# Loading the q and k weight chunks of a fused attention and FFN kernel as joint rows, with the first two tiles computed chunk by chunk over eight PSUM banks

## The chip, the cores and the metric

The kernel runs on one core of one Trainium2 chip (trn2). The metric is device time in microseconds (us); a lower time is better. Before the change it was 274.67 us (median of 3 runs, 274.52 to 274.93). The span in a profile, from the first to the last instruction, is about 1.3 us shorter than the device time of the same run (273.2 against 274.49 us for the kernel before).

Engines are named as the profile names them: PE is the TensorE matmul, PEld its weight load, DVE the vector engine, ACT the scalar engine, POOL GpSimd, SP the sync engine. SP and ACT each own a queue of loads ("SPq", "ACTq" in the profile when they issue one). The granted clock is the share of its full clock that PE is given, as the profile records it.

## The reference, cut to what matters

```python
# S = 2048, D = 640, H = 32 heads of 20, F = 1728
g = sigmoid((x * gate_w).sum(-1, keepdims=True))
q, k, v = split(x @ wqkv)                  # wqkv: 640 x 1920; q, k, v are 640 wide each
pq, pk = phi(q), phi(k)                    # phi(t) = where(t > 0, t + 1, exp(t)) + 1e-6
a = linear_attention(pq, pk, v) @ wo
b = (gelu(x @ w_gate) * (x @ w_up)) @ w_down
out = g * a + (1 - g) * b
```

The change touches only the start: the loads of the q and k columns of `wqkv`, and the products of the first two tiles (128 rows of x each) with them.

## The kernel before, as far as the change touches it

The 640 rows of `wqkv` are loaded in five chunks of 128 rows, and each matmul takes one chunk. A product of one tile with q or with k is a sum over five chunks, held in two banks of PSUM (the memory `ps`, where the results of PE go): 512 columns in one and 128 in the other. I call the two matmuls of one tile, one chunk and one of q or k a *step*; the first two tiles need 2 x 2 x 5 = 20 steps.

The loads before. k halves come first, chunk by chunk, with rows of 640 x 2 = 1280 bytes; q halves follow as two loads of two and three chunks:

```python
P.op("act", lambda e: e.dma_start(touch[0:16, 0:4], A_wqkv[0:128:8, 640:644]), ...)   # tiny "touch"
load_x(0)                # SP
load_wk(0)               # SP
load_x(1, "act")
load_wk(1)               # SP
load_wk(3)               # SP
...
load_wk(2, "act")
load_wk(4, "act")
...
dma_in(gw_sb[0:5, :], gate_w..., [r_gw], eng="act")     # gate weights, 1.2 KB
load_wq(0, 2)            # SP
load_wq(2, KC, "act")
for i in range(NXN, NT):                                # transposed x tiles 2 to 15, on SP
    load_xT(i, after=([r_wk[4]] if i == NXN else ()))
```

The products before: k of both tiles, in the order in which the chunks were expected, then q of both tiles.

```python
warm(5, 512); warm(1, 128)                 # matmuls on constants, to keep PE busy
T(0, [0], 7); T(0, [1, 2, 3, 4], 6)        # PE transposes of x tile 0
warm(6, 128)
KM(0, [0])                                 # step: k, tile 0, chunk 0
T(1, [0], 7); T(1, [1, 2, 3, 4], 6)
warm(3, 128)
KM(1, [0])
for k in (1, 3):
    KM(0, [k]); KM(1, [k])
gate_col()                                 # gate weights as an extra column of the q half
for k in (2, 4):
    KM(0, [k]); KM(1, [k])
for n in range(4):
    if n == 2:
        for k in range(3):
            QM(2, [k]); QM(3, [k])
        QM(2, [3, 4]); QM(3, [3, 4])
    phi1(n); phi2(n)                       # exp on ACT, then two operations on DVE
for i in range(2, NT):
    KQ(i)                                  # q and k of tiles 2 to 15
```

## Time and profile before

| what | before | read from |
|---|---|---|
| device time | 274.67 us | median of 3 runs |
| PE busy | 269.7 of 273.2 us | page, part 1 |
| PE waits after 11 us | none | waits of PE, window 11 us to the end |
| first matmul of KQ (tile 2) | 11.40 us | timeline of PE |
| chunk 3 of k lands, PE resumes | 6.96, 7.01 us | chain of waits, timeline |

From the page of the kernel before, its span, the busy times of part 1 and the shares of the chain that ended last:

```profile
span 273.2 us, 3449 instructions
...
PE 269.7 (99%) x1369; PEld 128.6 (47%) x1369; DVE 141.9 (52%) x251; ACT 76.0 (28%) x132; POOL 30.0 (11%) x28
...
PE 97%; DMA 2%; SPq 0%; DVE 0%; issue 0%
```

The kernel is PE-bound nearly from end to end. Only the head has idle PE time, and the chain that ended last shows what it waits for there. This is that chain in order of time (start, length, what):

```profile
2.21 4.76 DMA pool<-in_A_wqkv_dram
6.96 0.05 issue
7.01 0.39 PE ps L453
```

Up to 6.96 us the chain is a load of `wqkv`; from 7.01 us on it is PE without a break. The timeline of PE in the head (start, duration, operation; in brackets the idle time before it and what ended it):

```profile
4.62 0.38 PE L453 MATMUL ps<-pool 128*128 128x512 bf16 x1 [0.18 <-DMA pool<-in_A_wqkv_dram]
...
6.20 0.22 PE L454 MATMUL ps<-pool 128*128 128x128 bf16 x1
7.01 0.39 PE L453 MATMUL ps<-pool 128*128 128x512 bf16 x1 [0.59 <-DMA pool<-in_A_wqkv_dram]
7.23 0.22 PE L454 MATMUL ps<-pool 128*128 128x128 bf16 x1
7.29 0.38 PE L453 MATMUL ps<-pool 128*128 128x512 bf16 x1
...
11.40 0.81 PE L540 MATMUL ps<-pool 128*128 128x512 bf16 x3
```

L453 and L454 are the two matmuls of a k step. Steps start every 0.27 us (7.01, 7.29); the single durations are longer because matmuls overlap. There is one large wait, 0.59 us, for chunk 3 of k. The q steps that follow never wait. L540 is the first matmul of `KQ`. Since PE does not wait after it, its start decides the time.

### The profile page before, as it was taken

What the parts mean: (1) busy time and instruction counts of PE and PEld (TensorE: products, weight loads), DVE (VectorE), ACT (ScalarE), POOL (GpSimd) and SP (SyncE); (2) the same over time, 40 slices, a digit from 0 to 9 for tenths busy, and PEclk for the clock granted to TensorE, in tenths of its full rate; (3) what the DMA queues carried; (4) which work ended last, traced back from release to release, by engine and by line L of the source; (5) the groups of instructions that cost most, each with busy time, mean ns of one, the idle gap of its engine ahead of it and who ended that gap; (6) DMA issues with size and microseconds to landing.
All of it is one profiled execution on the core that took longest, in us unless ns stands there. A gap on an engine that the chain in (4) does not pass through costs nothing.

```text
span 273.2 us, 3449 instructions
## 1 busy us (share of the span) xinstructions
PE 269.7 (99%) x1369; PEld 128.6 (47%) x1369; DVE 141.9 (52%) x251; ACT 76.0 (28%) x132; POOL 30.0 (11%) x28
## 2 busy tenths in 40 slices
PE   7999999999999999999999999999999999999997
PEld 4555555544445444444444444444444444444444
DVE  2588989998234334999999999634210000000200
ACT  2355555310421454223222223224011121121021
POOL 5000000003240001242332422000000000000000
PEclk9999999999999999999999999999999999999999
DMA  6675999500300011522121221263031110110211
GB/s 207 179 118 122 322 402 386 143 3 12 65 19 2 23 49 51 182 45 48 26 48 24 48 42 34 60 215 109 5 77 38 41 38 19 38 41 19 58 58 41
DMA packets 42160, 23.61 MB, mean 86 GB/s; under 512 B 31519, under 2 KB 40735, under 8 KB 42015
## 3 DMA queue, kind: packets, MB, share of 16 engines
q1 hardware_dynamic: 41269, 22.40, 30.0%
q10 hardware_dynamic: 874, 0.98, 1.0%
q8 instruction: 11, 0.18, 0.3%
q14 instruction: 6, 0.05, 0.0%
HBM read 13.83 MB, written 2.63 MB: 60 GB/s over the span
## 4 chain that ended last, share of the span: by engine, by line
PE 97%; DMA 2%; SPq 0%; DVE 0%; issue 0%
PE ps L701 41%; PE ps L865 23%; PE ps L540 14%; PE ps L597 6%; PE ps L844 4%; DMA pool<-in_A_wqkv_dram 2%; PE ps L679 2%; PE ps L812 2%; PE ps L600 1%; PE ps L468 1%; PE ps L825 1%; PE ps L453 1%; PE ps L722 1%; PE ps L740 0%; SPq L340 0%; PE ps L469 0%
## 5 line engine op out<-in xcount | busy, mean ns | idle before, releaser
L701 PE MATMUL ps<-pool 128*128 128x512 bf16 x520 | 113.7, 379 | 0.0
L701 PEld LDWEIGHTS ps<-pool 128*128 128x128 bf16 x520 | 50.5, 98 | 60.0
L865 PE MATMUL ps<-pool 128*128 128x512 bf16 (+2 forms) x306 | 62.7, 367 | 0.0
L707 ACT ACTIVATE pool<-ps 128x512 f32<-128x512 f32 x52 | 31.0, 597 | 73.1 <-PE ps L701 73.1
L709 DVE TENSOR_TENSOR pool<-ps,pool 128x512 bf16<-128x512 f32 x52 | 34.7, 689 | 31.7 <-PE ps L701 30.4
L865 PEld LDWEIGHTS ps<-pool 128*128 128x128 bf16 x306 | 29.2, 98 | 33.4 <-issue 0.4
L540 PE MATMUL ps<-pool 128*128 128x512 bf16 (+1 forms) x210 | 38.1, 344 | 0.0
L848 DVE TENSOR_TENSOR pool<-ps,pool 128x512 bf16<-128x512 f32 x4 | 2.8, 692 | 61.5 <-PE ps L844 61.5
L755 POOL TENSOR_TENSOR pool<-pool 128x640 f32<-128x640 bf16 x16 | 22.5, 1406 | 72.9 <-DVE pool L757 66.2
L872 ACT ACTIVATE pool<-ps,pool 128x512 bf16<-128x512 f32 (+1 forms) x16 | 10.9, 681 | 68.6 <-PE ps L865 68.6
L540 PEld LDWEIGHTS ps<-pool 128*128 128x128 bf16 x210 | 20.5, 98 | 17.5
L559 DVE SCALAR_TENSOR_TENSOR pool<-ps,pool 128x128 bf16<-128x128 f32 (+2 forms) x42 | 25.3, 602 | 2.4
L550 ACT ACTIVATE pool<-ps 128x640 bf16<-128x640 f32 x28 | 19.7, 704 | 18.2 <-DVE pool L559 10.9
L597 PE MATMUL ps<-pool 128*128 128x512 bf16 x78 | 19.4, 379 | 0.0
L765 DVE TENSOR_TENSOR pool<-pool 128x640 bf16<-128x640 bf16 x16 | 13.2, 826 | 0.6
L763 DVE TENSOR_SCALAR pool<-pool 128x32 f32<-128x32 f32 x16 | 12.8, 802 | 0.6
L757 DVE TENSOR_REDUCE pool<-pool 128x32 f32<-128x640 f32 x16 | 12.9, 807 | 0.0
L645 DVE TENSOR_TENSOR pool<-pool 128x640 f32<-128x640 f32 x14 | 11.6, 825 | 0.5
L844 PE MATMUL ps<-pool 128*128 128x512 bf16 x52 | 11.6, 379 | 0.0
L647 POOL PARTITION_ALL_REDUCE pool<-pool x1 | 4.0, 3972 | 61.5 <-DVE pool L645 61.5
L597 PEld LDWEIGHTS ps<-pool 128*128 128x128 bf16 x78 | 7.0, 98 | 7.3
L556 DVE TENSOR_SCALAR pool<-pool 128x640 bf16<-128x640 bf16 x28 | 9.2, 327 | 1.8 <-ACT pool L550 0.3
(70 smaller groups left out, 105.8 us busy)
## 6 DMA issues: line engine op xcount, KB each, us to landing
out_dram<-pool SPq DMA_DIRECT2D x19, 128.0 KB, 1.7
pool<-in_B_w_gate_dram SPq DMA_DIRECT2D x1, 2080.0 KB, 13.8
pool<-in_B_w_up_dram SPq DMA_DIRECT2D x1, 2080.0 KB, 19.3
pool<-in_A_x_dram SPq DMA_DIRECT2D x1, 1280.0 KB, 8.6
pool<-in_B_w_down_dram SPq DMA_DIRECT2D x1, 1120.0 KB, 6.0
pool<-omg_row SPq DMA_DIRECT2D x1, 1024.0 KB, 4.8
pool<-in_A_x_dram SPq DMA_DIRECT2D x1, 960.0 KB, 5.7
pool<-in_A_wo_dram SPq DMA_DIRECT2D x6, 160.0 KB, 10.0
```

Source lines behind the costliest of these rows:

```text
L540: last = e.matmul(ps[:, b + p, 0:c1 - c0], xT[:, k, i * 128:(i + 1) * 128], wkq[:, k, c0:c1], start=(k == 0), stop=(k == KC - 1))
L550: P.op("act", lambda e: e.activation(e_buf[m], ps_flat[:, o:o + 640], ACT.Exp), reads=banks, writes=[r_e[m]])
L559: P.op("dve", lambda e, c0=c0, c1=c1: e.scalar_tensor_tensor(dst[:, c0:c1], ps_flat[:, o + c0:o + c1], 1.0 + EPS, e_buf[m][:, c0:c1], ALU. ...
L597: last = e.matmul(ps[:, b, :], pk[i][:, c * 128:(c + 1) * 128], x_aug[:, i, 0:512], start=(i == 0), stop=(i == NT - 1))
L701: last = e.matmul(ps[:, b, :], w[:, k, fc * 128:(fc + 1) * 128], xT[:, k, j * 512:(j + 1) * 512], start=(k == 0), stop=(k == KC - 1))
L707: P.op("act", lambda e: e.activation(ge[n], ps[:, gb, :], ACT.Gelu_apprx_tanh), reads=[bank[gb]], writes=[r_ge[n]])
L709: P.op("dve", lambda e: e.tensor_tensor(hT[fc][:, j * 512:(j + 1) * 512], ps[:, ub, :], ge[n], ALU.mult), reads=[bank[ub], r_ge[n]], write ...
L755: P.op("pool", lambda e: e.tensor_tensor(tmp[n], pq[i], z_b, ALU.mult), reads=[r_pq[i], r_zb], writes=[r_tmp[n]])
L757: P.op("dve", lambda e: e.tensor_reduce(den[n], tmp[n].rearrange("p (h d) -> p h d", h=32), AX.X, ALU.add), reads=[r_tmp[n]], writes=[r_de ...
L765: P.op("dve", lambda e: e.tensor_tensor(pq[i].rearrange("p (h d) -> p h d", h=32), pq[i].rearrange("p (h d) -> p h d", h=32), den[n].unsqu ...
L844: last = e.matmul(ps[:, b, :], wd[:, fc, 512:640], hT[fc][:, j * 512:(j + 1) * 512], start=False, stop=(fc == NFC - 2), skip_group_check=True)
L865: last = e.matmul(ps[:, pb, 0:c1 - c0], lhs, rhs, start=False, stop=(q == len(rows) - 1), skip_group_check=True)
```

## The change

The intent is to load q and k of a chunk together, as rows of 2560 bytes, so that fewer and longer rows are moved. Because q and k now arrive together, the first two tiles are computed chunk by chunk, with all four products open at once in all eight banks. A second tiny load, over chunks 1 to 4, is placed behind x tile 1 to touch that memory early. The gate load moves to the front, and the gate column moves from the q half to the k half. The core of the diff:

```diff
-            wk = wkq[:, :, 0:640]
-            wq = wkq[:, :, 640:1281]
+            wq = wkq[:, :, 0:640]
+            wk = wkq[:, :, 640:1281]
...
             load_x(0)
-            load_wk(0)
+            load_w(0, 640, 1280)
             load_x(1, "act")
-            load_wk(1)
-            load_wk(3)
+            P.op("act", lambda e: e.dma_start(touch[0:64, 4:8], A_wqkv[128:640:8, 640:644]), ...)
+            (the memset of gw_sb, moved here)
+            dma_in(gw_sb[0:5, :], gate_w.rearrange("(k p) -> k p", p=128), [r_gw], eng="act")
+            load_w(0, 0, 640)
+            load_w(1, 0, 1280)
+            load_w(3, 0, 1280)
...
-            load_wk(2, "act")
-            load_wk(4, "act")
-            dma_in(gw_sb[0:5, :], gate_w.rearrange("(k p) -> k p", p=128), [r_gw], eng="act")
-            load_wq(0, 2)
-            load_wq(2, KC, "act")
+            load_w(2, 0, 1280, "act")
+            load_w(4, 0, 1280, "act")
...
-                load_xT(i, after=([r_wk[4]] if i == NXN else ()))
+                load_xT(i, after=([r_wk[3]] if i == NXN else ()))
...
             warm(6, 128)
-            KM(0, [0])
+            PM(0, [0], tail=False)
             T(1, [0], 7)
             T(1, [1, 2, 3, 4], 6)
-            (warm(3, 128), then the k steps, the gate column and the q steps as above)
+            gate_col()
+            PM(1, [0], tail=False)
+            PM(0, [0], main=False)
+            PM(1, [0], main=False)
+            PM(2, [0])
+            PM(3, [0])
+            for n in range(4):
+                PM(n, [1])
             for n in range(4):
+                PM(n, [2])
+                PM(n, [3, 4])
                 phi1(n)
                 phi2(n)
```

`PM(n, ks)` does the steps of product n (k of tile 0, k of tile 1, q of tile 0, q of tile 1) over the chunks `ks`; "tail" is its second matmul, which for k also holds the gate column.

## The prediction

> **What bounds it now.** TensorE: the page gives PE 269.7 of 273.2 us, the chain of waits is 97% PE, and the waits of PE after 11 us are empty. The change acts only before that. What counts is the start of the first KQ matmul (L540, tile 2), 11.40 us in the timeline; any shift of it passes whole into the span.
>
> **The head now (timeline, and landings in the trace).** The first weight matmul is at 4.62 us (wk 0 lands at 4.49). 20 chunk steps (512 + 128 columns) follow at a pitch of 0.27 us, 5.4 us together. PE idles about 0.6 us, until 7.00, when wk 3 lands (6.96). wk 2 lands at 5.68, wk 4 at 7.16, the gate load at 7.35, wq 0-1 at 8.53, wq 2-4 at 9.39; wq is never late. So the order of now, wk first, hides most of the load. At most about 0.9 us is to be won.
>
> **What the change does.**
> - Rows of 2560 bytes. A 1280-byte packet takes 55 ns (median), a 3328-byte one of the later loads 133: about 6 ns fixed, so 2560 bytes should take 104 ns against 110. The Trainium skill (DMA: Bandwidth & Descriptors, "Why small descriptors are slow") names such a fixed cost; the trace agrees. On 1.3 MB that is about 0.2 us.
> - The second touch should take the long first packets (between 5.5 and 6.7 us many took 200 to 800 ns, and wk 3's last engine landed 1.0 us after its ninth). I count on half of that.
> - The gate load, ahead of the large loads, no longer lands at 7.35.
> - The cost: k and q of a chunk arrive together, so k is not served first. From 4.6 us 1.48 MB remain, as before. The same page ("Queues, rings and completion order") says that each engine alternates between queues; the trace shows both moving about equally from 3.3 to 5.5 us. At 350 to 380 KB/us (estimate from 332 now, less stalls and packet cost) the SP queue brings wq 0 at about 5.5, chunk 1 at 7.2, chunk 3 last at 8.6; the ACT queue chunk 2 at 6.5, chunk 4 at 8.3.
>
> **Critical path after.** Chunk 0's work ends at about 6.6 us. PE waits for chunk 1 until 7.2; from there 16 steps remain, 4.4 us: 11.6. From chunk 3's landing 11 remain, 3.0 us: 11.6. The transposed load of tile 2 starts when chunk 3 has landed, 8.6 instead of 7.17, and takes 2.95 us (measured now): 11.55, just in time. The release of banks 0 and 1 (1.9 us after a product's end now) comes at about 11.4. Four limits fall together; the latest decides: L540 starts at 11.5 to 11.9, estimate 11.65, 0.25 us later than now. Swapping the halves in KQ costs nothing: same matmuls, same vector work.
>
> **Prediction.** 274.67 + 0.25 = 274.9 us, 8 in 10 between 274.3 and 275.6. Faster by over 2%: 0.005; within 2%: 0.985; slower: 0.01.
>
> **What would show it.** Right: PE idle before chunk 1's matmuls (0.4 to 0.8 us) and again before chunk 3's or the first L540, released by DMA; after 12 us everything the same, shifted; the gate matmul no longer after the chunk 3 wait. Wrong: chunk 1 landing before 6.8 us or all chunks before 8.2 (all stalls gone), giving 274.3; or chunk 3 near 9.4 with the transposed load behind it, giving 275.5. A PE idle long enough to lower its granted clock (1.00 throughout now) would cost over 1 us; I give it 5%.

## The result

| | before | after |
|---|---|---|
| device time, median | 274.60 us (6 runs, 274.14 to 274.94) | 275.47 us (6 runs, 275.29 to 276.01) |
| span of the profiled run | 273.2 us | 274.0 us |
| first matmul of KQ | 11.40 us | 12.21 us |

The ratio of the runs is 1.0036 (95% interval 1.0021 to 1.0051). Ratios are the mean time of one kernel's fast runs over the mean time of the other's fast runs of the same rounds, so not quite the ratio of the medians quoted. The change made the kernel slower by 0.36%, which is about 1.0 us, clear of the noise though inside the band of 2%. A second measurement of the same kernel on another occasion gave 1.0036 again (below).

The page after, the same lines:

```profile
span 274.0 us, 3444 instructions
...
PE 270.5 (99%) x1366; PEld 128.7 (47%) x1366; DVE 141.8 (52%) x251; ACT 76.2 (28%) x132; POOL 30.0 (11%) x28
...
PE 96%; DMA 2%; ACTq 1%; ACT 0%; issue 0%; DVE 0%
```

The chain that ended last, after, in order of time:

```profile
3.46 5.62 DMA pool<-in_A_wqkv_dram
9.08 0.14 issue
9.22 0.38 PE ps L455
```

The load that the chain hangs on now lands at 9.08 us instead of 6.96. The timeline of PE, after (L455 and L457 are the two matmuls of a step, L524 is the first of KQ, L487 makes the gate column):

```profile
5.55 0.19 PE L487 MATMUL ps<-pool 128*128 128x5 bf16 x1 [0.20 <-DMA pool<-in_gate_w_dram]
5.60 0.59 PE L455 MATMUL ps<-pool 128*128 128x512 bf16 x1
...
7.09 0.39 PE L455 MATMUL ps<-pool 128*128 128x512 bf16 x1
...
8.40 0.39 PE L455 MATMUL ps<-pool 128*128 128x512 bf16 x1
8.62 0.22 PE L457 MATMUL ps<-pool 128*128 128x129 bf16 x1
9.22 0.38 PE L455 MATMUL ps<-pool 128*128 128x512 bf16 x1 [0.38 <-DMA pool<-in_A_wqkv_dram]
...
12.21 2.10 PE L524 MATMUL ps<-pool 128*128 128x512 bf16 x9
```

PE waits for the gate weights (5.55), for chunk 1 (7.09), for chunk 2 (8.40, one step) and for chunk 4 (9.22). From 9.22 us on it is gapless, and 11 of the 20 steps are still to be done: 12.21 - 9.22 = 2.99 us.

The matmul at 5.60 took 0.59 us, where those of the kernel before took 0.38 from 4.62 us on: PE was still at half pace. In all fourteen profiles the first matmuls of 512 columns start every 0.43 us and later ones every 0.22. The pace doubles at 4.2 us in the kernel before, at about 6.3 us in the changed kernel, and between 3.9 (e9) and 9.8 us (e3) in the other runs, although the windows view gives a granted clock of 1.00 from the start. This did not decide the time here: in the second profile of the changed kernel PE was at full pace from 4.7 us on, and KQ started later still (12.47 us), because the last landing decided.

When each load landed, from the completion records in the trace (us; a load is complete when the last of its sixteen shares has landed). "After, again" is the second profile of the changed kernel:

| load | before | after | after, again |
|---|---|---|---|
| chunk 0 | k 4.49 | k 4.08, q 4.84 | k 4.08, q 4.77 |
| chunk 1 | k 5.46 | 7.05 | 7.56 |
| chunk 2 | k 5.68 | 8.35 | 8.36 |
| chunk 3 | k 6.96 | 8.34 | 9.06 |
| chunk 4 | k 7.16 | 9.08 | 9.34 |
| gate weights | 7.35 | 5.51 | 6.33 |
| q chunks 0 and 1 | 8.53 | with the chunks | with the chunks |
| q chunks 2 to 4 | 9.39 | with the chunks | with the chunks |

This table holds the explanation to be tested. The last byte came a little *sooner* after the change (9.08 against 9.39 us). But before, when the last load (q 2 to 4) landed, PE was still working on q chunks 0 and 1, with only 6 steps to go from 9.76 us, and did not wait. After, 11 steps stood behind the last landing.

### The profile page after: what moved, and what is told of

It is laid out like the page before. It is cut to its first block, busy times and chain, and to the rows that moved or that the text cites. A ratio compares the mean times of both kernels' runs of the same rounds, so it can differ in the third digit from the quotient of the medians.

```text
span 274.0 us, 3444 instructions
## 1 busy us (share of the span) xinstructions
PE 270.5 (99%) x1366; PEld 128.7 (47%) x1366; DVE 141.8 (52%) x251; ACT 76.2 (28%) x132; POOL 30.0 (11%) x28
## 4 chain that ended last, share of the span: by engine, by line
PE 96%; DMA 2%; ACTq 1%; ACT 0%; issue 0%; DVE 0%
PE ps L685 41%; PE ps L849 23%; PE ps L524 14%; PE ps L581 6%; PE ps L828 4%; DMA pool<-in_A_wqkv_dram 2%; PE ps L796 2%; PE ps L663 2%; PE ps L584 1%; PE ps L455 1%; PE ps L809 1%; PE ps L706 1%; PE ps L724 0%; ACTq L340 0%; PE ps L457 0%; ACTq L360 0%
## 5 line engine op out<-in xcount | busy, mean ns | idle before, releaser
L524 PE MATMUL ps<-pool 128*128 128x512 bf16 (+1 forms) x210 | 38.1, 344 | 0.0
L524 PEld LDWEIGHTS ps<-pool 128*128 128x128 bf16 x210 | 20.5, 98 | 17.5
L629 DVE TENSOR_TENSOR pool<-pool 128x640 f32<-128x640 f32 x14 | 11.6, 826 | 0.5
L828 PE MATMUL ps<-pool 128*128 128x512 bf16 x52 | 11.6, 379 | 0.0
```

The source lines that it names most:

```text
L524: last = e.matmul(ps[:, b + p, 0:c1 - c0], xT[:, k, i * 128:(i + 1) * 128], wkq[:, k, c0:c1], start=(k == 0), stop=(k == KC - 1))
L828: last = e.matmul(ps[:, b, :], wd[:, fc, 512:640], hT[fc][:, j * 512:(j + 1) * 512], start=False, stop=(fc == NFC - 2), skip_group_check=True)
```

## The experiments

Theory A: the cost is the arrival order. With q and k of a chunk in one load, no product can finish its sum before nearly all bytes have come, so too many steps are left behind the last landing. Its rivals: B, the small loads early on the ACT queue delay chunks 2 and 4; C, the release of banks or the transposed load of tile 2 is the limit; D, long rows stall more; E, the eight-bank order itself costs.

Each experiment was timed over 5 rounds against the kernel before on the same chip (4 to 6 runs of each). The table gives the ratio to the kernel before and, for the profiled run, the start of the first KQ matmul and the span.

| run | edited from | ratio (95% interval) | KQ starts | span |
|---|---|---|---|---|
| changed kernel | | 1.0036 (1.0021 to 1.0051) | 12.21 | 274.0 |
| after_again | after, unchanged | 1.0036 (1.0020 to 1.0052) | 12.47 | 274.2 |
| e1_no_touch2 | after | 1.0066 (1.0037 to 1.0095) | 15.03 | 276.8 |
| e2_pool_small | after | 1.0121 (1.0106 to 1.0135) | 15.04 | 276.8 |
| e3_chunk2_all | after | 1.0054 (1.0035 to 1.0073) | 13.90 | 275.7 |
| e4_half_rows | after | 1.0038 (1.0026 to 1.0050) | 12.52 | 274.3 |
| e5_k_then_q | after | 1.0090 (1.0061 to 1.0118) | 12.00 | 273.8 |
| e9_k_first | after | 1.0011 (0.9998 to 1.0024) | 11.60 | 273.4 |
| e10_small_sp | after | 1.0069 (1.0048 to 1.0089) | 12.63 | 274.4 |
| e7_before_touch2 | before | 1.0029 (1.0013 to 1.0044) | 12.03 | 273.9 |
| e6_before_k_order | before | 0.9990 (0.9978 to 1.0001) | 11.18 | 272.9 |
| e8_before_q_single | before | 0.9970 (0.9955 to 0.9984) | 11.71 | 273.5 |
| e12_q_single_only | before | 0.9993 (0.9979 to 1.0007) | 10.81 | 272.6 |

One thing can be read from the last two columns at once. From the first KQ matmul to the end, all fourteen profiles (these and the kernel before) take 261.7 to 261.9 us, however the head went. So everything that separates these kernels happens before KQ, and it passes whole into the time. A profile is one run; where the runs of a kernel differ among themselves, its ratio counts and its profile shows only how that one run went. The profiles of e1, e3 and e8 are of runs near or at the slow end of their kernel (278.02, 276.92 and 274.85 us, medians 275.98, 276.13 and 273.90), that of e5 is of its fastest (275.00, median 277.43).

### Undoing the grouping of the loads (e9_k_first)

```diff
-            load_w(0, 0, 640)
-            load_w(1, 0, 1280)
-            load_w(3, 0, 1280)
+            load_w(1, 640, 1280)
+            load_w(3, 640, 1280)
...
-            load_w(2, 0, 1280, "act")
-            load_w(4, 0, 1280, "act")
+            load_w(2, 640, 1280, "act")
+            load_w(4, 640, 1280, "act")
+            (then q chunks 0 and 1 on SP, q chunks 2 to 4 on ACT)
...
             (PE: the k steps over chunks 1, 3, 2, 4, then the q steps, as before the change)
```

> The changed kernel with only the load grouping and the PE order put back: k halves of all chunks first (1280-byte rows), q halves last, k products before q products; second touch, early gate load, gate column in the k half and the swapped halves all kept. Theory A (k and q arriving together is the cost): back to before, first KQ matmul near 11.4 us, ratio 0.999 to 1.001. Rival B (small loads early on the ACT queue are the cost): stays near the changed kernel, ratio 1.003 or more, chunk 2 and 4 of k late.

Measured: 274.76 us against 274.36 for the kernel before, ratio 1.0011, interval 0.9998 to 1.0024, at the edge of what theory A had expected and far from B. The second touch, the early gate load and the swapped halves are all still in this kernel. PE still had some short waits. These are the last of them and the start of KQ (L530 here):

```profile
9.95 0.39 PE L458 MATMUL ps<-pool 128*128 128x512 bf16 x1 [0.17 <-DMA pool<-in_A_wqkv_dram]
...
11.60 2.65 PE L530 MATMUL ps<-pool 128*128 128x512 bf16 x13
```

The last q load landed at 9.91 us in this run, later than any load of the changed kernel in its profile, and yet KQ started 0.6 us sooner, since only 6 steps waited for that load. Theory A is confirmed for most of the loss, if one goes by the middle of the intervals (0.25 of 0.36%); between 0 and about 0.24% can still belong to what was kept.

### Undoing only the PE order (e5_k_then_q)

```diff
             PM(1, [0], main=False)
-            PM(2, [0])
-            PM(3, [0])
-            for n in range(4):
-                PM(n, [1])
-            for n in range(4):
-                PM(n, [2])
-                PM(n, [3, 4])
-                phi1(n)
-                phi2(n)
+            for c in (1, 3, 2, 4):
+                PM(0, [c])
+                PM(1, [c])
+            (phi of both k products)
+            for c in (0, 1, 2, 3, 4):
+                PM(2, [c])
+                PM(3, [c])
+            (phi of both q products)
```

> The changed kernel's loads (k and q of a chunk together), but PE in the order of before: k products over all chunks, then q products. Theory A: the eight-bank order is not the cost but the remedy; without it 12 steps instead of 11 wait for the last chunk and none of the q work fills the waits, first KQ matmul 0.3 to 0.8 us later than in the changed kernel, ratio 1.004 to 1.007. Rival E (the eight-bank order itself costs): ratio back at 1.000 to 1.002.

Measured: 277.43 us, ratio 1.0090, more than expected. The six runs fall in two groups: 275.00 and 276.07 us, with a mean granted clock of 1.000, and 277.38 to 277.75 us, with 0.994. The eight-bank order is therefore not the cost (rival E falls): the changed kernel's runs (275.29 to 276.01 us) are like the good runs of the old order, and none of them falls in the other group, which the next experiment explains. Together with e9 this puts the cost on the loads: the kernels of e5 and e9 differ in nothing but the grouping and order of these loads, were timed in the same rounds on the same chip, and have the ratios 1.0090 and 1.0011. No run of e9 is over 274.99 us, and none of e5 is under 275.00.

### Taking the second touch away (e1_no_touch2)

```diff
-            P.op("act", lambda e: e.dma_start(touch[0:64, 4:8], A_wqkv[128:640:8, 640:644]), ...)
```

> The changed kernel without its second small load (touch of chunks 1 to 4). Theory A (arrival order: k and q come together, so 11 chunk steps, 3.0 us, are left when the last chunk lands): the second touch is not the cause; the chunk 2 and 4 loads are issued 0.5 us earlier, first KQ matmul within 0.3 us of 12.2 us, ratio to before 1.002 to 1.005. Rival B (the small loads at the head of the ACT queue delay chunks 2 and 4): chunk 2 and 4 land about 0.5 us earlier and the first KQ matmul starts at about 11.7 us, ratio 1.001 to 1.002. If the touch does what it was made for, long packets get more and it is slower than the changed kernel.

Measured: ratio 1.0066, six runs from 275.06 to 278.02 us. Rival B's gain did not come, and the ratio is above theory A's range too. In the profiled run chunk 1 had a straggler: its ninth share landed at 5.56 us and its last at 9.08. PE waited over 2 us for it, and its clock fell. Below are the timeline of PE and the windows view (stretch, its length, then busy time with number of instructions per engine, then granted clock, DMA share and GB/s) of this run:

```profile
6.75 0.22 PE L455 MATMUL ps<-pool 128*128 128x128 bf16 x1
9.12 0.61 PE L453 MATMUL ps<-pool 128*128 128x512 bf16 x1 [2.16 <-DMA pool<-in_A_wqkv_dram]
9.52 0.32 PE L455 MATMUL ps<-pool 128*128 128x129 bf16 x1
9.63 0.63 PE L453 MATMUL ps<-pool 128*128 128x512 bf16 x1
```

```profile
7.00:8.00 1.00, 0.00 (x0) 0.00 (x0) 0.00 (x0) 0.00 (x0) 0.00 (x0) 1.00 0.83 282
8.00:9.00 1.00, 0.00 (x0) 0.00 (x0) 0.00 (x0) 0.00 (x0) 0.00 (x0) 0.95 0.37 143
9.00:10.00 1.00, 0.88 (x3) 0.39 (x4) 0.00 (x0) 0.00 (x0) 0.00 (x0) 0.50 0.17 69
```

After the wait a step takes 0.51 to 0.53 us instead of 0.27, until about 12.3 us: the granted clock is half. The Trainium skill (TensorE: Matmul & The Clock Gate, Part 1) describes a clock that falls to half after an idle window of about 3.4 us and returns after a busy window of about the same length. The length agrees: the trace records the fall at 8.89 us and the return at 12.31. But the fall came only 1.9 us after the last matmul before the wait had ended (6.97 us). Half the clock for 3.4 us costs about 1.7 us (an estimate from these times), and a mean clock of 0.994 over 277 us is one such stretch. So a late chunk can cost twice: first the wait, then the slow clock.

That the touch protects the loads from stragglers is not shown. Two of the six runs without it lost their clock; the other four (275.06 to 276.17 us) are like those of the changed kernel, and the intervals overlap. The profile has no more long packets than those of the changed kernel (14 of over 200 ns started between 4.5 and 7 us, against 16 and 24), and chunk 1 had a straggler with the touch too: in the second profile of the changed kernel its ninth share landed at 5.43 and its last at 7.56 us.

### Moving the small loads off the ACT queue (e2_pool_small, e10_small_sp)

```diff
-            (second touch and gate load on ACT)
+            (second touch and gate load on POOL, behind the identity)
```

> The changed kernel with both small loads (second touch, gate column) issued by the POOL engine instead of ACT, so chunk 2 and 4 loads are issued at 1.7 and 2.1 us instead of 3.1 and 3.5. Theory A: the bytes before the last chunk are the same, all land by 8.7 to 9.1 us, first KQ matmul at 11.7 to 12.2 us, ratio 1.001 to 1.004. Rival B: chunk 2 lands by 6.5 and chunk 4 by 8 us as predicted, first KQ matmul at 11.3 us or earlier, ratio 0.999 to 1.000.

Measured: ratio 1.0121, four runs all with a mean clock of 0.994. The timing says nothing on A against B, because I had made a new wait: the gate load issued from POOL came so late that PE stood 2.53 us for it, until 7.99 us, and lost its clock as in e1:

```profile
7.99 0.18 PE L487 MATMUL ps<-pool 128*128 128x5 bf16 x1 [2.53 <-DMA pool<-in_gate_w_dram]
```

The landings are of use all the same: chunk 2 at 6.26, chunk 1 at 8.16, chunk 4 at 8.37 and chunk 3 at 8.85 us. Chunks 2 and 4 were issued 1.3 us earlier than in the changed kernel and landed 2.1 and 0.7 us earlier; chunks 1 and 3, on the SP queue, were issued as before (2.19 and 2.66 us) and yet landed 1.1 and 0.5 us later. The last landing of all moved by 0.2 us only. With the gate weights in time, the 16 steps behind chunk 1 would still have ended at about 8.2 + 4.4 = 12.6 us (an estimate from these landings), no sooner than in the changed kernel. The second try puts both small loads on SP:

```diff
             load_w(0, 640, 1280)
+            dma_in(gw_sb[0:5, :], gate_w.rearrange("(k p) -> k p", p=128), [r_gw])
+            P.op("sp", lambda e: e.dma_start(touch[0:64, 4:8], A_wqkv[128:640:8, 640:644]), ...)
             load_x(1, "act")
-            (second touch and gate load on ACT)
```

> The changed kernel with gate load and second touch issued on the SP queue after the first k half, so the ACT queue carries only x tile 1, chunk 2 and chunk 4, issued at 1.7 and 2.1 us (3.1 and 3.5 in the changed kernel). Theory A: chunk 2 lands near 6.3 and chunk 4 near 8.4 us as predicted, but chunk 1 and 3 later for it (8.2 and 8.8 us), first KQ matmul at 11.8 to 12.5 us, ratio 1.002 to 1.005. Rival B: first KQ matmul at 11.4 us or earlier, ratio 1.000 or less.

Measured: ratio 1.0069, above both ranges. Chunk 2 landed at 5.34 and chunk 4 at 7.07 us, 3.0 and 2.0 us earlier than in the changed kernel; chunk 1 landed at 8.22 and chunk 3 at 9.01, later by 1.2 and 0.7 us, and the q half of chunk 0 at 7.40. PE in this run:

```profile
7.45 0.39 PE L455 MATMUL ps<-pool 128*128 128x512 bf16 x1 [1.16 <-DMA pool<-in_A_wqkv_dram]
...
8.26 0.39 PE L455 MATMUL ps<-pool 128*128 128x512 bf16 x1
...
12.63 1.67 PE L524 MATMUL ps<-pool 128*128 128x512 bf16 x7
```

From chunk 1 on, 16 steps at 0.27 us: 8.26 + 4.37 = 12.63. This run alone does not separate the theories, because the small loads now hold up the SP queue: chunks 1 and 3 were issued at 3.36 and 3.83 us instead of 2.18 and 2.65. Two of its six runs also lost their clock (0.994), and PE kept its order although chunk 4 lay ready. Together with the landings of e2, where the SP queue was left alone, it says that freeing the ACT queue moves the lateness to the other queue, so rival B does not explain the loss. This agrees with the Trainium skill (DMA: Bandwidth & Descriptors, "Issuing engines are not separate DMA queues"), which says that loads issued by different engines run on the same sixteen DMA engines and that issuing from several saves only the time of issuing.

### The touch in the kernel before (e7_before_touch2)

```diff
             load_x(1, "act")
+            P.op("act", lambda e: e.dma_start(touch[0:64, 4:8], A_wqkv[128:640:8, 640:644]), ...)
             load_wk(1)
```

> The kernel before with only the second touch added behind x tile 1 on the ACT queue. Theory A with the touch taking some long first packets but costing one ACT issue of 0.5 us: within 0.1% of before, ratio 0.999 to 1.001, chunk 3 of wk landing no later than 7.0 us. Rival B: the chunk 2 and 4 loads come 0.5 us later and PE waits for them, ratio 1.002 or more.

Measured: ratio 1.0029, outside what theory A had expected and in line with B. In its profile the loads behind the touch on the ACT queue are late: k chunk 2 at 7.43 us (5.68 before), k chunk 4 at 8.28 (7.16), the gate weights at 8.13 (7.35), and PE waited for k chunk 3 and for the gate weights:

```profile
7.30 0.39 PE L455 MATMUL ps<-pool 128*128 128x512 bf16 x1 [0.25 <-DMA pool<-in_A_wqkv_dram]
...
8.18 0.18 PE L500 MATMUL ps<-pool 128*128 128x5 bf16 x1 [0.17 <-DMA pool<-in_gate_w_dram]
```

Chunks 2 and 4 came in time for PE all the same; chunk 3 is on the SP queue, which the touch does not hold up, and was late by its last share (7.25 us, the ninth 5.20). In this profile, then, only the wait for the gate weights is B's mechanism. By the ratio, an extra small load ahead of large ones costs about 0.8 us in the old arrangement. In e9, which has the same touch, this did not show: there the gate load is ahead of the large loads, and the SP queue brought k chunk 3 at 5.51 and q chunks 0 and 1 at 7.59 us (6.96 and 8.53 before). Which of these differences saves e9 was not separated.

### The length of the rows (e4_half_rows)

```diff
-            load_w(1, 0, 1280)
-            load_w(3, 0, 1280)
+            load_w(1, 640, 1280)
+            load_w(1, 0, 640)
+            load_w(3, 640, 1280)
+            load_w(3, 0, 640)
             (chunks 2 and 4 on ACT likewise)
```

> The changed kernel with each 2560-byte-row load split into two loads of 1280-byte rows (k half, then q half), same queues and same order. Rival D (the long rows stall more: packets of 600 to 1000 ns were seen at 4.6 us): 0.3 us or more faster than the changed kernel. Theory A, with long rows 6% cheaper per byte (102 against 2 x 55 ns): the last chunk lands 0.1 to 0.3 us later, ratio 1.0035 to 1.005.

Measured: ratio 1.0038, against 1.0036. Row length, the stated purpose of the change, makes no difference that can be seen here, either way; rival D falls. Nor does it help to split the loads while their order and that of PE stay: here the k half of each chunk is a load of its own and nothing is won. A packet of 2560 bytes did take 102 ns (median) in the changed kernel against 55 ns for 1280 bytes, so the 7% are real, but they are small beside the long packets described below.

### Filling the wait for chunk 4 (e3_chunk2_all)

```diff
             for n in range(4):
                 PM(n, [2])
+            for n in range(4):
                 PM(n, [3, 4])
```

> The changed kernel; PE does chunk 2 for all four products before it asks for chunks 3 and 4. In the changed kernel PE idled 0.6 us between 8.6 and 9.2 us for chunk 4 while three chunk-2 steps were ready. Theory A: these fill the wait: first KQ matmul 0.5 us earlier (11.7 us), ratio about 1.002. Rival C (the limit is the release of PSUM banks by the vector work, or the transposed load of tile 2): no gain, ratio 1.0035.

Measured: ratio 1.0054, no gain; its fastest run (275.38 us) is no faster than the fastest of the changed kernel (275.29). The profiled run, a slow one, shows two reasons. PE ran its steps at 0.53 us until about 9.8 us, with the clock not yet up although the windows view gives it as 1.00; and the first KQ matmul (L525) then had to wait for a bank:

```profile
13.21 0.22 PE L457 MATMUL ps<-pool 128*128 128x128 bf16 x1
13.90 0.39 PE L525 MATMUL ps<-pool 128*128 128x512 bf16 x1 [0.47 <-DVE pool L481]
```

Doing chunk 2 for all four products ends the first product later, so its phi ends later (the DVE operation L481 ran from 13.02 to 13.84 us), and KQ needs that bank at once. A part of what is won on PE is thus given back at the bank; this is rival C, turned from a limit of the changed kernel into one of this variant. How much each reason weighs over all six runs is open.

### The changed kernel once more (after_again)

> The changed kernel once more, on this chip and in the same rounds as the other two: ratio 1.0025 to 1.005 again; its trace shows whether the late landings of chunks 2 and 4 (8.4 and 9.1 us) and the PE waits come again: first KQ matmul at 12.0 to 12.6 us.

Measured: 275.70 us against 274.52, ratio 1.0036. The waits came again with other sizes: 1.24 us for the gate weights, 0.34 us for the last chunk (9.48 us), then 11 steps to 12.47 us.

### Does the theory yield a faster kernel? (e6_before_k_order, e8_before_q_single, e12_q_single_only)

If it is the number of steps behind each landing that counts, the kernel before can be improved in the opposite direction: finer loads in the order of use. Its PE took chunk 3 before chunk 2, though chunk 2 landed 1.3 us earlier, and its q came in loads of two and three chunks.

```diff
-            for k in (1, 3):
+            for k in (1, 2, 3):
                 KM(0, [k]); KM(1, [k])
             gate_col()
-            for k in (2, 4):
+            for k in (4,):
```

> The kernel before, PE takes the k chunks in the order 1, 2, 3, 4 instead of 1, 3, 2, 4 (chunk 2 landed at 5.68 us, chunk 3 at 6.96 where PE waited). The 0.6 us wait shrinks to about 0.2, but the first q load lands at 8.5 us all the same, so the q products start there: first KQ matmul at 11.3 us instead of 11.4, ratio 0.999 to 1.000. If PE's k waits alone set the time: 10.95 us, ratio 0.998.

Measured: ratio 0.9990, interval 0.9978 to 1.0001; KQ started at 11.18 us, with a wait of 0.54 us for q chunks 0 and 1. As expected, the wait moved from k to q.

```diff
             (e6, and:)
-            load_wq(0, 2)
-            load_wq(2, KC, "act")
+            load_wq(0, 1)
+            load_wq(1, 2, "act")
+            load_wq(2, 3)
+            load_wq(3, 4, "act")
+            load_wq(4, 5)
...
-                    QM(2, [3, 4])
-                    QM(3, [3, 4])
+                    for k in (3, 4):
+                        QM(2, [k])
+                        QM(3, [k])
```

> The same and in addition the q chunks loaded one by one, alternating SP and ACT queue, instead of as two loads of 2 and 3 chunks, so that each q chunk can be used as it lands. Theory A (what counts is how many chunk steps are left behind each landing): q 0 lands by 7.9 us, no wait for q, first KQ matmul at 10.8 to 11.1 us, ratio 0.997 to 0.999, faster than both kernels. If bytes alone count: q 4 last at 9.4 us and no change, ratio 1.000.

Measured: 273.90 us against 274.52, ratio 0.9970, interval 0.9955 to 0.9984. This kernel beats both. Its profile fell on its slowest run (274.85 us), in which the last share of most loads came late (k chunk 1: ninth share at 4.91, last at 6.73 us), so it shows KQ only at 11.71. The other five runs lie between 273.48 and 274.24 us.

> The kernel before with only the q chunks loaded one by one on both queues, the k order 1, 3, 2, 4 kept. Of the 0.3% that both edits gained, the order alone had shown 0.1% (its interval holds 0). Theory A (PE waited for the two-chunk q load only after the k work is done, so a gain in k and a gain in q need each other): ratio 0.997 to 0.999, wait for q gone in the trace, wait for k chunk 3 still there. If the q loads gain nothing alone: 1.000.

The q loads alone (the second diff, with its order of the last q steps, without the first): ratio 0.9993, interval 0.9979 to 1.0007. Its profiled run, 273.97 us against a median of 274.38 for the kernel before, went well: no wait for q is left, the wait for k chunk 3 that was expected to stay is gone too (it landed at 6.38 us already), and KQ starts at 10.81 us:

```profile
6.42 0.39 PE L456 MATMUL ps<-pool 128*128 128x512 bf16 x1
...
10.81 1.46 PE L544 MATMUL ps<-pool 128*128 128x512 bf16 x6
```

Neither edit is clear of zero alone, both together are. That they need each other is plausible but not shown, as the three intervals overlap.

## Why the prediction was right or wrong

It forecast 274.9 us (274.3 to 275.6) and a small loss; measured were 275.47 us and a loss of about 1.0 us instead of 0.25. The direction and the mechanism were right, the size was too small.

- *A shift of the first KQ matmul passes whole into the span.* Right: fourteen profiles have 261.7 to 261.9 us from there to the end.
- *The cost is that k and q of a chunk arrive together and k is not served first.* Right, by e9 against e4, e5 and e10.
- *2560-byte packets take 104 ns.* Right (102 ns), but worth nothing that can be seen (e4).
- *The second touch takes half of the long packets.* Wrong. Between 4.5 and 7 us the changed kernel had 16 packets of over 200 ns, as many as the kernel before (its second profile had 24). Compared with the old loads nothing was gained; whether it would have been worse without the touch is open (e1). The windows view shows the hole in the stretch from 5 to 6 us. First the kernel before, then the kernel after; the last number is GB/s:

```profile
5.00:6.00 1.00, 1.00 (x14) 0.67 (x12) 0.65 (x2) 0.00 (x0) 0.00 (x0) 1.00 1.02 302
```

```profile
5.00:6.00 1.00, 0.80 (x6) 0.22 (x3) 0.76 (x3) 0.00 (x0) 0.00 (x0) 1.00 0.87 231
```

- *Landings of 7.2, 6.5, 8.6 and 8.3 us for chunks 1 to 4.* This is the term that failed: 7.05, 8.35, 8.34 and 9.08 us. The chunks of the ACT queue were mis-sized. I had left out that the touch and the gate load hold up that queue: chunks 2 and 4 were issued at 3.09 and 3.5 us instead of 1.79 and 2.2. But in e2 an earlier issue made chunks 1 and 3 late instead and brought the last landing only to 8.85 us, so by these landings (one profile) most of the error is in the rate. I expected 350 to 380 KB/us; by packets ended, the changed kernel moved 1192 KB from 4.6 to 8.5 us (306 KB/us), the kernel before 1220 KB (313 KB/us). My 1.48 MB "remaining at 4.6 us" was too much as well, because it counted only finished loads (1.20 MB came between 4.6 us and the last landing); the two errors partly cancelled.
- *PE is idle 0.4 to 0.8 us before chunk 1.* It was idle only from 6.95 to 7.09 us. It came to chunk 1 later than forecast, because it had waited for the gate weights and had run at half pace until about 6.3 us.
- *From the last landing 11 steps remain, 3.0 us.* Right: 2.99 us, from 9.22 to 12.21. The sum was 8.6 + 3.0 = 11.6; it should have been 9.2 + 3.0 = 12.2.
- *The transposed load of tile 2 and the release of the banks come just in time.* Right, they did not decide: the first landed at 11.25 us, and the first phi ended at 11.96, both before 12.21. The bank did decide in e3.
- *The granted clock falls, 5%.* It did not in the changed kernel (mean clock 1.0 in every run listed), but it did in e1, e2, e5 and e10, where a chunk or the gate load came some microseconds late. These variants suggest that the changed kernel is nearer to that edge than the kernel before; no run of either shows it. The "1.00 throughout" of the prediction is what the view gives; by the pace of the matmuls the kernel before also starts at half clock, until 4.2 us.

## What to carry to other kernels

When a stage waits for loads, do not ask when the last byte comes but how much work stands behind each landing: a load that serves two products at once ties both to its last share, while half loads in the order of use let one product finish during the transfer of the other. Both orders, that of the loads and that of the matmuls, have to fit: splitting the loads alone (e4) won nothing. Doubling 1280-byte rows was worth nothing measurable here, and a freed issue slot on one queue was paid for by the loads of the other (e2). Before a profile's granted clock is believed, the pitch of equal matmuls should be looked at. A matmul engine that waits over two microseconds at the start (2.16 and 2.53 us here) may then also run at half clock, so a late load can cost twice.

## What the Trainium skill lacked or had wrong

- TensorE: Matmul & The Clock Gate (Part 1 and "Why this matters for your kernels"): its rule is to leave no idle gap of more than about 3 us. In e1 the clock fell to half for 3.4 us with a wait of 2.16 us, soon after the start; in e2 with one of 2.53 us. The page also says that the window runs free of the kernel's start, but not how busy PE must be within it to keep the clock. The records of e1 change at 5.48, 8.89 and 12.31 us, in steps of 3.4 us; in the stretch from 5.48 to 8.89 PE was busy for 1.26 us, and for 0.80 us in that of e2 (4.89 to 8.30), and both were followed by half the clock.
- The same page warns that recorded clock events are not to be trusted blindly. The view gave 1.00 from the start in every profile, while PE ran at half pace until 3.9 (e9) to 9.8 us (e3), and in five of the fourteen (changed kernel twice, e7, e8, e12) the trace has no record of the change. The pitch of equal matmuls is the better witness.
- DMA: Bandwidth & Descriptors ("Queues, rings and completion order" and "Why a DMA increments its semaphore by 16 and not by 1") says that a load is complete only with all of its shares, but gives no size for the spread between them. Here the last share of a chunk came 1.6 us after the ninth in the changed kernel (chunk 1: 5.43 and 7.05 us), and 3.5 us after it in e1.
- The same page ("Latency and other measured facts") gives 0.2 us on average and up to 2 us at high load for an HBM access. Single 2560-byte packets took up to 1.02 and 1.45 us in the two profiles of the changed kernel and 1.34 us in e3, inside that range, against a median of 102 ns. No page read says that the first loads of a kernel are prone to this, or whether a touch load helps. That is open here too: e1 does not settle it, and in e7 the touch cost about 0.8 us where large loads queue behind it.
